# Feed-forward on blocks of 1024 tokens: seven products of halves, and the second product with the weights stationary

## The chip, the cores and the metric

The kernel runs on one core of a Trainium2 chip. The core has a matmul engine (PE, with its weight loads shown as PEld), a vector engine (DVE), a scalar engine (ACT), a general engine (POOL), an engine that issues most of the DMA transfers (SP), and 16 DMA engines. The metric is device time in microseconds (us).

## The reference

Three layers follow each other: an attention with squared ReLU, a mixture of eight experts of which each token takes one, and a feed-forward. Only the last is changed:

```python
def _moe2_ref(x, w_in, w_out):            # x: 24576 x 256, w_in: 256 x 2048, w_out: 2048 x 256
    h = x @ w_in
    g = h * (1.0 / (1.0 + np.exp(-h)))
    return (g @ w_out).astype(np.float32)
```

## The kernel before

The work runs in three stages: attention, experts, feed-forward. Within a stage the order of the instructions is written by hand, as a loop over iterations g in which each engine's instructions are recorded in the order in which they are to run. An engine takes its instructions in that order. Waits between engines are put in by the tile layer, which tracks who read and wrote a tile.

A number is kept as the sum of a high part, rounded to the matmul's format (fp32r), and a low part, the rest. A product of two such numbers is taken as three products: high x high, high x low, low x high. `split` (line 147) makes the two parts: ACT copies, DVE subtracts.

The feed-forward takes blocks of 512 tokens (CB) and, in each iteration, 256 of the 2048 columns of the first product; a block has 8 iterations, the stage 48 x 8 = 384. `emit_H` (line 903) multiplies: for each of two groups of 128 columns and each of two halves of the inner dimension of 256, three matmuls of 512 columns (lines 911 to 913), with a weight as the stationary operand. The result stands in PSUM, tile `hps`. `elem_c` (line 1122) computes the sigmoid on ACT, the product with it on DVE, the high part on ACT and the low part on DVE, each over 1024 columns at once. `emit_AV_c` (line 1132) multiplies by the second weight: here the activations are the stationary operand, and high and low weight lie side by side, so a matmul of 512 columns (lines 236, 239) gives the products with both; the low activations take matmuls of 256 columns (237, 238). The first product runs two iterations ahead of the second (`pipeline_c`, line 1092), and eight PSUM banks hold two `hps` tiles of two banks and four accumulators.

`load_c` (line 1112) loads a block of the input by four DMAs on SP's queue in pieces of 256 bytes, `tr_x` (858) transposes it on DVE, `ev_x` (866) splits it, all several iterations ahead. `evac_c` (line 1137) adds the two halves of an accumulator, and SP stores the block by one DMA.

The second weights arrive as 64-bit numbers; `plan_cw` (line 980) converts both weights to high and low parts during the expert stage, one or two instructions in an iteration, into tiles with pads between them (`CPAD`).

Of the kernel before, what the change touches and what calls it, by code (L numbers as in the profile page):

```python
# [20 lines left out]
def relu2_attention__moe_top1__silu_ffn_kernel(  # L21
# [12 lines left out]
):  # L34

# [43 lines left out]
    CB = 512  # L79
    CT = CB // P  # L80
    NCB = N // CB
    GP = DFF // P // 2

# [43 lines left out]
    X2 = nc.dram_tensor("x2_scratch", (N, D), F32, kind="Internal").ap()  # L127
    TS = [nc.dram_tensor(f"ts{i}_scratch", (P, 2 * QN), F32, kind="Internal").ap() for i in range(3)]
# [95 lines left out]
    def at(g, fn):  # L224
        bg.setdefault(g, []).append(fn)
# [740 lines left out]
    CPAD = (0, 64, 224, 192)  # L966

    def start_c():

        only_a.close()  # L970
        pool = cw["pool"] = ctx.enter_context(tc.tile_pool(name="poolC", bufs=1))
        cw["wih"], cw["wil"], cw["wo"] = [], [], []
        for q in range(4):
            if CPAD[q]:
                pool.tile([P, CPAD[q] // 4], F32, name=f"cpad{q}")
            cw["wih"].append(pool.tile([P, KD, DFF // 4], F32R, name=f"wih{q}"))
            cw["wil"].append(pool.tile([P, KD, DFF // 4], F32R, name=f"wil{q}"))
            cw["wo"].append(pool.tile([P, DFF // P // 4, 2, D], F32R, name=f"wo{q}"))

    def plan_cw(g, src, dst):  # L980
# [10 lines left out]
        def hi(d=I32):  # L991
            return h["raw"].bitcast(d)[:, :, :, 1]
# [7 lines left out]
        def field():  # L1000
# [30 lines left out]
    def plan_cws(g):  # L1031
        for i in range(GP):
            q, o = divmod(i, GP // 4)
            fs = slice(o * 2 * P, (o + 1) * 2 * P)
            cs = slice(2 * o, 2 * o + 2)
            plan_cw(g, w_in_v[:, :, i * 2 * P:(i + 1) * 2 * P, :],
                    lambda q=q, fs=fs: (cw["wih"][q][:, :, fs], cw["wil"][q][:, :, fs]))
            plan_cw(g + 6, w_out_v[:, 2 * i:2 * i + 2],
                    lambda q=q, cs=cs: (cw["wo"][q][:, cs, 0, :], cw["wo"][q][:, cs, 1, :]))
            g += 12  # L1040

    NAB = NIT + NIB
    plan_cws(NIT + 24)
# [48 lines left out]
    def pipeline_c(lo, hi):  # L1092
        g = min(bg)
        while g < hi:
            ahead = g + 2 if lo <= g + 2 < hi else None
            if ahead is not None:
                s = emit_S_c(ahead)
            run(bg, g)
            if g >= lo:
                emit_AV_c(g)  # L1100
            if ahead is not None:
                rest = elem_c(ahead, s)
            if g >= lo:
                evac_c(g)
            if ahead is not None:
                rest()
            g += 1


    XC = {}  # L1110

    def load_c(b):
        XC[b] = mt("y", [P, 4 * CT, 64], F32, "xc")
        load_rows(XC[b], CT, X2[b * CB:(b + 1) * CB])

    def emit_S_c(g):
        b, i = divmod(g, GP)
        q, o = divmod(i, GP // 4)
        fs = slice(o * 2 * P, (o + 1) * 2 * P)
        return emit_H(XT[b], cw["wih"][q][:, :, fs], cw["wil"][q][:, :, fs], CB)  # L1120

    def elem_c(g, ps):
        s = mt("r1", [P, 2, CB], F32, "sg")
        a = mt("r2", [P, 2, CB], F32, "ga")
        A.activation(out=s, in_=ps, func=AF.Sigmoid)  # L1125
        V.tensor_tensor(out=a, in0=ps, in1=s, op=ALU.mult)  # L1126
        h = hi_t[g] = mt("h", [P, 2, CB], F32R, "gh")
        l = lo_t[g] = mt("l", [P, 2, CB], F32R, "gl")
        A.activation(out=h, in_=a, func=AF.Copy)  # L1129
        return lambda: V.tensor_tensor(out=l, in0=a, in1=h.bitcast(F32), op=ALU.subtract)  # L1130

    def emit_AV_c(g):
        b, i = divmod(g, GP)
        q, o = divmod(i, GP // 4)
        emit_acc(g, CT, [flat(cw["wo"][q], 2 * o + f) for f in range(2)], i == 0, i == GP - 1)

    def evac_c(g):
        b, i = divmod(g, GP)
        if i < GP - 1:
            return  # L1140
        o = mt("u", [P, CT, D], F32, "oc")
        for j in range(CT):
            acc = acc_t.pop(j)
            t1 = mt("t1", [P, D], F32, "t1")
            A.activation(out=t1, in_=acc[:, D:2 * D], func=AF.Copy)
            V.tensor_tensor(out=o[:, j], in0=acc[:, 0:D], in1=t1, op=ALU.add)
        SP.dma_start(out=out[b * CB:(b + 1) * CB].rearrange("(j p) d -> p j d", p=P), in_=o)

    with tc.manual_schedule():
# [8 lines left out]
        for b in range(NCB):  # L1158
            g = b * GP
            at(g - 10, lambda b=b: load_c(b))  # L1160
            at(g - 6, lambda b=b: tr_x(XC.pop(b), CT, b, by=KD if b else 1))
            at(g - 5, lambda b=b: ev_x(CT, b, KD if b else 1))
        pipeline_c(0, NCB * GP)
# [32 lines left out]
```

## Time and profile before

| | |
|---|---|
| median of three runs | 5356.03 us (5354.76 to 5363.61) |
| the profiled execution | 5354.29 us, span 5352.3 us |
| attention / experts / feed-forward start at about | 0 / 2034 / 3208 us |
| PE busy in the span | 99% |
| DVE, ACT busy in the span | 65%, 57% |
| feed-forward: first matmul, last matmul | 3208.27, 5346.91 us |

Times are from the span's start. A matmul's shown length includes its way through the engine, so matmuls overlap; what one costs PE is the distance from its start to the start of the next. "Idle before" names what ended an engine's wait.

### The profile page before, as it was taken

The page shows a single profiled execution, that of the slowest core. Times are in us where ns is not written, and L with a number is a line of the kernel's source. Part 1 is how long each engine was busy: PE and PEld are TensorE (multiplying, and loading weights), DVE is VectorE, ACT ScalarE, POOL GpSimd, SP SyncE. Part 2 cuts the span into 40 slices and gives each one's busy share as a digit, 9 for nine tenths or more (in the row PEclk, how much of TensorE's full clock was granted, in tenths as well). Part 3 has the DMA queues.
Part 4 walks back from the last instruction along what each step waited for, and adds up shares of the span by engine and source line. Part 5 has one row for each costly group of instructions (what it writes and reads, how often), then busy time and mean ns, then how long its engine had stood idle before and what let it go on. Part 6 is the DMA issues. An engine that isn't in the chain of part 4 may idle for free.

```text
span 5352.3 us, 77144 instructions
## 1 busy us (share of the span) xinstructions
PE 5280.5 (99%) x29600; PEld 4589.1 (86%) x29600; DVE 3496.2 (65%) x4352; ACT 3055.0 (57%) x4010; POOL 752.1 (14%) x977
## 2 busy tenths in 40 slices
PE   8999999999999999999999999999999999999999
PEld 7888889898989897888888888888888888888888
DVE  6777777777786878777766665555555555555554
ACT  7777777777777875555555554444444444444444
POOL 1131322222222313111111120000000000000000
PEclk9999999999999999999999999999999999999999
DMA  5556565556565556655544550000000000000000
GB/s 149 174 171 182 167 186 165 177 169 185 170 177 172 175 176 190 179 160 160 158 141 142 142 150 17 24 24 24 24 24 24 24 24 24 24 24 24 24 24 20
DMA packets 711601, 588.06 MB, mean 110 GB/s; under 512 B 372892, under 2 KB 629951, under 8 KB 711232
## 3 DMA queue, kind: packets, MB, share of 16 engines
q1 hardware_dynamic: 539200, 458.63, 28.8%
q10 hardware_dynamic: 152928, 73.95, 5.5%
q0 software_dynamic: 19104, 50.56, 2.6%
q8 instruction: 231, 3.78, 0.3%
q14 instruction: 138, 1.13, 0.1%
HBM read 364.89 MB, written 207.59 MB: 107 GB/s over the span
## 4 chain that ended last, share of the span: by engine, by line
PE 69%; issue 17%; DMA 7%; ACT 2%; DVE 2%; POOL 2%; SPq 1%; ACTq 0%; POOLq 0%; DVEq 0%
PE acc L236 11%; PE acc L239 11%; PE hps L912 7%; PE hps L911 7%; PE hps L913 7%; PE acc L238 6%; PE acc L237 6%; PE acct L697 4%; PE acct L698 4%; PE acct L699 4%; DMA x_scratch<-y,gi 2%; DMA ts_scratch<-tb 2%; PE s L642 2%; PE s L643 2%; DMA at<-ts_scratch 2%
## 5 line engine op out<-in xcount | busy, mean ns | idle before, releaser
L1126 DVE TENSOR_TENSOR ga<-hps,sg 128x1024 f32<-128x1024 f32 x384 | 470.3, 1225 | 578.0 <-ACT sg L1125 578.0
L1125 ACT ACTIVATE sg<-hps 128x1024 f32<-128x1024 f32 x384 | 394.5, 1027 | 739.8 <-PE hps L913 739.8
L1130 DVE TENSOR_TENSOR gl<-ga,gh 128x1024 fp32r<-128x1024 f32 x384 | 470.1, 1224 | 379.8 <-ACT gh L1129 379.8
L1129 ACT ACTIVATE gh<-ga 128x1024 fp32r<-128x1024 f32 x384 | 407.3, 1061 | 496.2 <-DVE ga L1126 496.2
L911 PE MATMUL hps<-xh,wih 128*128 128x512 f32 x1536 | 605.8, 394 | 10.0 <-ACT xh L148 10.0
L913 PE MATMUL hps<-xh,wil 128*128 128x512 f32 x1536 | 605.9, 394 | 0.0
L912 PE MATMUL hps<-xl,wih 128*128 128x512 f32 x1536 | 605.9, 394 | 0.0
L236 PE MATMUL acc<-wo,gh 128*128 128x512 f32 x1536 | 604.4, 394 | 0.0
L239 PE MATMUL acc<-wo,gh 128*128 128x512 f32 x1536 | 602.8, 392 | 0.0
L697 PE MATMUL acct<-vs,th 128*128 128x256 f32 x1920 | 542.9, 283 | 17.8 <-DVE xg L704 17.0
L698 PE MATMUL acct<-vs,th 128*128 128x256 f32 x1920 | 541.8, 282 | 0.0
L699 PE MATMUL acct<-vs,tl 128*128 128x256 f32 x1920 | 541.4, 282 | 0.0
L239 PE MATMUL acc<-vs,ah 128*128 128x512 f32 x1344 | 532.8, 396 | 0.0
L236 PE MATMUL acc<-vs,ah 128*128 128x512 f32 x1344 | 532.3, 396 | 0.0
L664 DVE TENSOR_TENSOR al<-a,ah 128x1024 fp32r<-128x1024 f32 x336 | 408.9, 1217 | 107.4 <-ACT ah L657 104.4
L651 ACT ACTIVATE a<-s 128x1024 f32<-128x1024 f32 x336 | 342.5, 1019 | 185.0 <-PE s L643 160.8
L238 PE MATMUL acc<-wo,gl 128*128 128x256 f32 x1536 | 429.8, 280 | 0.0
L237 PE MATMUL acc<-wo,gl 128*128 128x256 f32 x1536 | 428.6, 279 | 0.0
L927 ACT ACTIVATE hh<-hps 128x1024 fp32r<-128x1024 f32 (+1 forms) x220 | 213.9, 972 | 343.6 <-PE hps L913 295.9
L928 DVE SCALAR_TENSOR_TENSOR hl<-hps,hh 128x1024 fp32r<-128x1024 f32 (+1 forms) x220 | 254.3, 1156 | 231.1 <-ACT hh L927 229.3
L662 DVE STREAM_TRANSPOSE tb<-a 128x1024 f32<-128x1024 f32 x240 | 297.5, 1240 | 133.1 <-ACT a L653 130.0
L697 PEld LDWEIGHTS acct<-vs,th 128*128 128x128 f32 x1920 | 364.9, 190 | 22.3 <-DVE xg L704 21.1
(224 smaller groups left out, 13053.0 us busy)
## 6 DMA issues: line engine op xcount, KB each, us to landing
ts_scratch<-tb SPq DMA_DIRECT2D x240, 512.0 KB
at<-ts_scratch SPq DMA_DIRECT2D x960, 128.0 KB
r<-in_moe_w_dram SPq DMA_DIRECT2D x220, 512.0 KB
vr<-in_v_dram ACTq DMA_DIRECT2D x48, 512.0 KB
ut<-in_u_dram ACTq DMA_DIRECT2D x48, 512.0 KB
xb<-xs_scratch SPq DMA_DIRECT2D x192, 128.0 KB
xc<-x_scratch SPq DMA_DIRECT2D x192, 128.0 KB
out_dram<-oc SPq DMA_DIRECT2D x48, 512.0 KB
```

Of the source, the lines that this page charges most:

```text
L236: T.matmul(acc, lhsT=hs[0], rhs=ws[0], start=start, stop=False)
L237: T.matmul(acc[:, D:2 * D], lhsT=ls[0], rhs=ws[0][:, 0:D], start=False, stop=False)
L238: T.matmul(acc[:, D:2 * D], lhsT=ls[1], rhs=ws[1][:, 0:D], start=False, stop=False)
L239: T.matmul(acc, lhsT=hs[1], rhs=ws[1], start=False, stop=stop)
L697: T.matmul(acc[:, kk], lhsT=lh, rhs=vq[:, 0], start=(q == 0), stop=False)
L698: T.matmul(acc[:, kk], lhsT=lh, rhs=vq[:, 1], start=False, stop=False)
L699: T.matmul(acc[:, kk], lhsT=ll, rhs=vq[:, 0], start=False, stop=(q == QT - 1))
L911: T.matmul(o, lhsT=a, rhs=xh[:, d], start=(d == 0), stop=False)
L912: T.matmul(o, lhsT=a, rhs=xl[:, d], start=False, stop=False)
L913: T.matmul(o, lhsT=wl[:, d, f * P:(f + 1) * P], rhs=xh[:, d], start=False, stop=(d == KD - 1))
L1126: V.tensor_tensor(out=a, in0=ps, in1=s, op=ALU.mult)
L1130: return lambda: V.tensor_tensor(out=l, in0=a, in1=h.bitcast(F32), op=ALU.subtract)
```

## The change

The feed-forward takes blocks of 1024 tokens as two halves of 512 (index t), the 2048 columns as two halves of 1024, and the inner dimension as two halves of 128. The first product is then a product of 2 x 2 matrices of blocks, and is taken by seven products of sums instead of eight. With A for the weight's quarters and B for the input's:

- S1 = A21 + A22, S2 = S1 - A11, S3 = A11 - A21, S4 = A12 - S2 for the weight; T1 = B12 - B11, T2 = B22 - T1, T3 = B22 - B12, T4 = B21 - T2 for the input;
- M1 = A11 B11, M2 = A12 B21, M6 = S2 T2, M7 = S3 T3, M5 = S1 T1, M3 = S4 B22, M4 = A22 T4, each three matmuls of 512 columns (`emit_M`);
- H11 = M1 + M2; H22 = M1 + M6 + M5 + M7; H12 = M1 + M6 + M5 + M3; H21 = M1 + M6 + M7 + M4. M1, M6, M5 and M3 add up in one PSUM bank, Q; ACT copies what stands there on the way (`copy`, C[0] to C[2]), and DVE adds a copy to the bank R (M2) or Z (M7, then M4).

An iteration, called a step below, does this for 1024 tokens and 128 columns out of each half, and the second products of the step before; there are 24 x 8 = 192 steps. Q is one half of the tile `m0`, the other half in the next step; R and Z are the halves of the tile `m1`. The eight banks are these four and four accumulators. Sigmoid, product, high and low part are now taken of each 512-column quarter (H11, H22, H21, H12) apart.

The second product takes the weight as the stationary operand and the activations as the moving one, so its result is transposed: six matmuls of 512 columns for each quarter, into accumulators of 128 output columns by 512 tokens. `evac_c` transposes them out of PSUM on DVE, and eight DMAs a block store pieces of 256 bytes. The input's sums, transposes and splits for the next block are spread over a block's eight steps (`prep_c`). The weight's sums are computed in the expert stage after the conversions (`plan_sums`); S2, S3 and S4 go through memory into tiles that the expert stage has done with. The pads between the weights are gone.

```diff
-    CB = 512
-    CT = CB // P
+    CB = 1024
+    CH = CB // 2
...
+    def plan_sums(g):
...
+            def add(x, k):
+                o = h[x] = mt("a", [P, FH], F32R, f"s{x}") if k == 1 else h[x]
+                first = quarter(x, terms[0][1]) if k == 1 else o
+                V.tensor_tensor(out=o.bitcast(F32), in0=first.bitcast(F32), in1=quarter(x, terms[k][1]).bitcast(F32),
+                                op=ALU.add if terms[k][0] > 0 else ALU.subtract)
...
+            ops = [lambda x=x, k=k: add(x, k) for k in range(1, len(terms)) for x in range(2)]
+            for op in [*ops, high, rest, low_part, *([store] if to else [])]:
+                at(g, op)
+                g += 1
...
-    def emit_S_c(g):
+    def prep_c(b):
+
+        return [[], [lambda: load_c(b)], [lambda: tr_c(b, 0), lambda: tr_c(b, 1)],
+                [lambda: sum_c(0), lambda: sum_c(1)], [lambda: sum_c(2), lambda: sum_c(3)],
+                [lambda: parts_c(b, 1)], [lambda: parts_c(b, 2)], [lambda: parts_c(b, 0)], [lambda: parts_c(b, 3)]]
...
+    def emit_M(g, name, o, start=True):
...
+        T.matmul(o, lhsT=wh, rhs=xh, start=start, stop=False, skip_group_check=True)
+        T.matmul(o, lhsT=wh, rhs=xl, start=False, stop=False, skip_group_check=True)
+        T.matmul(o, lhsT=wl, rhs=xh, start=False, stop=True, skip_group_check=True)
...
+        for d in range(2):
...
+            o = acc_c[b, d, t]
+            wh, wl = (cw["o"][:, f * GP + i, y, d * P:(d + 1) * P] for y in range(2))
+            T.matmul(o, lhsT=wh, rhs=x[:, 0], start=start, stop=False)
+            T.matmul(o, lhsT=wh, rhs=x[:, 1], start=False, stop=False)
+            T.matmul(o, lhsT=wl, rhs=x[:, 0], start=False, stop=stop)
...
+    def pipeline_c():
+        s0 = psS.tile([P, 2, CH], F32, tag="s0", name="m0", bufs=1)
+        s1 = psS.tile([P, 2, CH], F32, tag="s1", name="m1", bufs=1)
...
+            Q, R, Z = s0[:, g % 2], s1[:, 0], s1[:, 1]
...
+            if now:
+                emit_M(g, "M1", Q)
+            if old:
+                high(g - 1, "H12")
+                low_part(g - 1, "H22")
+            if now:
+                copy(0, Q)
+                emit_M(g, "M2", R)
+            if old:
+                low_part(g - 1, "H12")
+                mul("H21")
+                high(g - 1, "H21")
+            if now:
+                add("H11", 0, R)
+            if old:
+                low_part(g - 1, "H21")
+                emit_AV_c(g - 1, "H11")
+            if now:
+                sig("H11")
+                mul("H11")
+                emit_M(g, "M6", Q, False)
+                copy(1, Q)
+                high(g, "H11")
+                emit_M(g, "M7", Z)
+            for fn in todo:
+                fn()
+            if now:
+                low_part(g, "H11")
+            if old:
+                emit_AV_c(g - 1, "H22")
+            if now:
+                emit_M(g, "M5", Q, False)
+                copy(2, Q)
+            if old:
+                emit_AV_c(g - 1, "H21")
+            if now:
+                add("H22", 2, Z)
+                sig("H22")
+                emit_M(g, "M3", Q, False)
+                emit_M(g, "M4", Z, False)
+            if end:
+                evac_c(b - 1, 0, 0)
+            if now:
+                sig("H12", Q)
+                mul("H22")
+                high(g, "H22")
+            if end:
+                evac_c(b - 1, 0, 1)
+            if now:
+                add("H21", 1, Z)
+                mul("H12", Q)
+                sig("H21")
+            if old:
+                emit_AV_c(g - 1, "H12")
```

PE's instructions before, in the middle of the feed-forward, at the end of a second product and the start of a first one; names with numbers are single tiles, and the bracket names the engine whose semaphore the instruction waits for:

```order
L237 MATMUL acc_48704<-wo2_24244,gl_48802 128x256
L238 MATMUL acc_48704<-wo2_24244,gl_48802 128x256
L239 MATMUL acc_48704<-wo2_24244,gh_48801 128x512
L911 MATMUL hps_48883<-xh_48493,wih3_24246 128x512 [waits DVE_49]
L912 MATMUL hps_48883<-xl_48494,wih3_24246 128x512
L913 MATMUL hps_48883<-xh_48493,wil3_24247 128x512
```

The first product's tile had been read by DVE an iteration earlier. Now PE's instructions at the end of a step in the middle of the feed-forward: M4, the second products of H12 of the step before, and M1 of the next step.

```order
L1207 MATMUL m1_35699<-xp_41915,wih_24234 128x512 [waits DVE_49]
L1208 MATMUL m1_35699<-xp_41916,wih_24234 128x512
L1209 MATMUL m1_35699<-xp_41915,wil_24235 128x512
L1233 MATMUL acc_42017<-g_42208,wo_24236 128x512
L1234 MATMUL acc_42017<-g_42208,wo_24236 128x512
L1235 MATMUL acc_42017<-g_42208,wo_24236 128x512
L1233 MATMUL acc_42021<-g_42208,wo_24236 128x512
L1234 MATMUL acc_42021<-g_42208,wo_24236 128x512
L1235 MATMUL acc_42021<-g_42208,wo_24236 128x512
L1207 MATMUL m0_35698<-xp_41840,wih_24234 128x512 [waits DVE_49]
L1208 MATMUL m0_35698<-xp_41841,wih_24234 128x512
L1209 MATMUL m0_35698<-xp_41840,wil_24235 128x512
```

M1 in the tenth row waits for DVE; the value of the semaphore that it waits for is reached by DVE's product for H12 (line 1273, out of `m0`), the fourth row of the next piece. DVE's instructions before, in the middle of the feed-forward:

```order
L1126 TENSOR_TENSOR ga_47747<-hps_47713,sg_47746 128x1024 [waits Activation_49]
L1130 TENSOR_TENSOR gl_47751<-ga_47747,gh_47750 128x1024 [waits Activation_49]
L1126 TENSOR_TENSOR ga_47784<-hps_47754,sg_47783 128x1024 [waits Activation_49]
L1130 TENSOR_TENSOR gl_47788<-ga_47784,gh_47787 128x1024 [waits Activation_49]
L862 STREAM_TRANSPOSE xt_47804<-xc_47633 128x16x2x32 [waits DMAHW6_49,DMAHW5_49,DMAHW7_49,DMAHW1_49,DMAHW0_49]
```

And now, from M5 of the same step to the sum for H11 of the next: the sum for H22, its product with the sigmoid, the sum for H21, the product for H12, two low parts, the product for H21, the sum for H11.

```order
L1267 TENSOR_TENSOR hs_35701<-m1_35699,hs_35700 128x512 [waits Activation_49]
L1273 TENSOR_TENSOR sg_35705<-hs_35701,sg_35705 128x512 [waits Activation_49]
L1267 TENSOR_TENSOR hs_35700<-m1_35699,c_35703 128x512 [waits PE_49]
L1273 TENSOR_TENSOR sg_35707<-m0_35698,sg_35707 128x512 [waits Activation_49]
L1283 TENSOR_TENSOR g_42268<-sg_35705,g_42268 128x512 [waits Activation_49]
L1283 TENSOR_TENSOR g_42282<-sg_35707,g_42282 128x512 [waits Activation_49]
L1273 TENSOR_TENSOR sg_35706<-hs_35700,sg_35706 128x512
L1267 TENSOR_TENSOR hs_35701<-m1_35699,c_35702 128x512 [waits PE_49,Activation_49]
```

Two instructions of 1024 columns in an iteration have become eleven of 512 in a step, and the sum for H21 (third row) waits for M4.

## Rows read from the trace of the kernel before

**Rows 1.** The page: busy time of the engines, and shares of the chain:
```profile
PE 5280.5 (99%) x29600; PEld 4589.1 (86%) x29600; DVE 3496.2 (65%) x4352; ACT 3055.0 (57%) x4010; POOL 752.1 (14%) x977
...
PE 69%; issue 17%; DMA 7%; ACT 2%; DVE 2%; POOL 2%; SPq 1%; ACTq 0%; POOLq 0%; DVEq 0%
```

**Rows 2.** Windows: feed-forward, experts, experts later; us, busy us by engine:
```profile
core 0: us, PE busy (x) PEld busy (x) DVE busy (x) ACT busy (x) POOL busy (x), PEclk, DMA share, GB/s
4000.00:5000.00 1000.00, 1000.00 (x5033) 843.37 (x5033) 520.98 (x496) 421.26 (x474) 0.00 (x0) 1.00 0.09 24
2560.00:2920.00 360.00, 360.00 (x1834) 306.24 (x1833) 253.28 (x349) 190.19 (x287) 66.23 (x64) 1.00 0.52 149
2740.00:2900.00 160.00, 160.00 (x815) 136.09 (x814) 99.39 (x130) 81.55 (x122) 28.43 (x28) 1.00 0.49 139
```

**Rows 3.** Timeline of PE in the feed-forward: start us, us, what:
```profile
4000.75 0.39 PE L911 MATMUL hps<-xh,wih 128*128 128x512 f32 x1
...
4003.32 0.39 PE L913 MATMUL hps<-xh,wil 128*128 128x512 f32 x1
4003.55 0.40 PE L236 MATMUL acc<-wo,gh 128*128 128x512 f32 x1
...
4006.33 0.39 PE L911 MATMUL hps<-xh,wih 128*128 128x512 f32 x1
```

**Rows 4.** Timeline of ACT and DVE in the same stretch:
```profile
4003.81 1.03 ACT L1125 ACTIVATE sg<-hps 128x1024 f32<-128x1024 f32 x1 [2.20 <-PE hps L913]
4004.87 1.23 DVE L1126 TENSOR_TENSOR ga<-hps,sg 128x1024 f32<-128x1024 f32 x1 [2.00 <-ACT sg L1125]
4006.12 1.06 ACT L1129 ACTIVATE gh<-ga 128x1024 fp32r<-128x1024 f32 x1 [1.29 <-DVE ga L1126]
4007.22 1.23 DVE L1130 TENSOR_TENSOR gl<-ga,gh 128x1024 fp32r<-128x1024 f32 x1 [1.13 <-ACT gh L1129]
```

**Rows 5.** Groups by form on DVE: count | busy us, mean ns | idle before:
```profile
L704 DVE TENSOR_TENSOR xg<-xg,acct 128x512 f32<-128x512 f32 x240 | 164.0, 684 | 110.7 <-PE acct L699 94.0 <-PE acct L499 11.3 <-PE acct L583 4.0
L149 DVE TENSOR_TENSOR w1l<-r,w1h 128x512 fp32r<-128x512 f32 x220 | 150.7, 685 | 1.2 <-ACT w1h L148 0.9
L862 DVE STREAM_TRANSPOSE xt<-xc 128x1024 f32<-128x1024 f32 x47 | 58.1, 1237 | 0.0
```

**Rows 6.** Groups by form on ACT:
```profile
L148 ACT ACTIVATE w1h<-r 128x512 fp32r<-128x512 f32 x220 | 137.1, 623 | 1.9 <-DMA r<-in_moe_w_dram 1.9
```

**Rows 7.** Timeline of DVE in the expert stage, back to back:
```profile
3170.50 0.69 DVE L149 TENSOR_TENSOR w1l<-r,w1h 128x512 fp32r<-128x512 f32 x1
3171.10 0.69 DVE L149 TENSOR_TENSOR w<-r,w 128x512 fp32r<-128x512 f32 x1
```

**Rows 8.** Timeline of ACT in the expert stage, back to back:
```profile
3169.51 0.62 ACT L148 ACTIVATE w1h<-r 128x512 fp32r<-128x512 f32 x1
3170.03 0.62 ACT L148 ACTIVATE w<-r 128x512 fp32r<-128x512 f32 x1
```

**Rows 9.** Timeline at the end of the feed-forward, PE and ACT:
```profile
5345.51 0.39 PE L239 MATMUL acc<-wo,gh 128*128 128x512 f32 x1
5345.94 0.38 ACT L1145 ACTIVATE t<-acc 128x256 f32<-128x256 f32 x1 [0.32 <-PE acc L239]
```

**Rows 10.** Timeline of the attention, DVE and PE, where PE waits:
```profile
510.65 0.68 DVE L704 TENSOR_TENSOR xg<-xg,acct 128x512 f32<-128x512 f32 x1
...
511.38 0.39 PE L697 MATMUL acct<-vs,th 128*128 128x256 f32 x1 [1.58 <-DVE xg L704]
511.60 0.28 PE L698 MATMUL acct<-vs,th 128*128 128x256 f32 x1
511.72 0.27 PE L699 MATMUL acct<-vs,tl 128*128 128x256 f32 x1
...
794.75 0.50 PE L642 MATMUL s<-st 128*128 128x512 f32 x1 [1.82 <-ACT a L651]
795.08 0.40 PE L643 MATMUL s<-sw,st 128*128 128x512 f32 x1
```

**Rows 11.** Windows: first load of the feed-forward, a store and a load:
```profile
3203.00:3212.00 9.00, 3.73 (x8) 2.71 (x9) 2.60 (x4) 1.22 (x2) 0.00 (x0) 0.50 0.77 175
3308.00:3314.00 6.00, 6.00 (x32) 5.03 (x31) 3.43 (x3) 2.16 (x3) 0.00 (x0) 1.00 0.67 178
```

**Rows 12.** Timeline at the start of the feed-forward:
```profile
3206.84 1.30 DVE L862 STREAM_TRANSPOSE xt<-xc 128x512 f32<-128x512 f32 x2 [7.55 <-DMA xc<-x_scratch]
...
3208.27 0.79 PE L911 MATMUL hps<-xh,wih 128*128 128x512 f32 x1 [10.00 <-ACT xh L148]
...
3211.30 0.63 PE L911 MATMUL hps<-xh,wih 128*128 128x512 f32 x1
3211.72 0.63 PE L912 MATMUL hps<-xl,wih 128*128 128x512 f32 x1
```

**Rows 13.** Timeline at the end, PE and SP:
```profile
5346.91 0.39 PE L239 MATMUL acc<-wo,gh 128*128 128x512 f32 x1
5348.21 0.37 SPq L1147 DMA_DIRECT2D out_dram<-oc  x1
```

More of the change, by code (lines that the diff above doesn't have):

```diff
@@ L964, in relu2_attention__moe_top1__silu_ffn_kernel @@
     cw = {}
-    CPAD = (0, 64, 224, 192)
     def start_c():
@@ L1090, in pipeline_ab @@
             g += 1
[L1092 to L1107, printed above, removed]
@@ L1132, in emit_AV_c @@
-    def emit_AV_c(g):
-        b, i = divmod(g, GP)
[L1134 to L1147, printed above, removed]
+    XC, XF, TC = {}, {}, {}
@@ new lines, in parts_c @@
+    def parts_c(b, n):
+        if n == 3:
+            h, l = (mt("st", [P, CH], F32R, "xp", x) for x in range(2))
+        elif n == 1:
+            h, l = (mt("a" if b % 2 == 0 else "xh", [P, KD, CH], F32R, "xp") for x in range(2))
+        else:
+            h, l = (mt("w2" if n else "xl", [P, KD, CH], F32R, "xp", 2 * (n and b % 2) + x) for x in range(2))
+        split(h, l, TC[n])
+        if n == 3:
+            XF["T4"] = h, l
+        else:
+            for k, name in enumerate((("B11", "B21"), ("T3", "B22"), ("T1", "T2"))[n]):
+                XF[b % 2 if n else 0, name] = h[:, k], l[:, k]
@@ new lines, in relu2_attention__moe_top1__silu_ffn_kernel, with rooms_c, emit_AV_c @@
+    QUADS = dict(H11=(0, 0), H22=(1, 1), H21=(1, 0), H12=(0, 1))
+    quads, acc_c, out_c, room = {}, {}, {}, {}
+    def rooms_c():
+        x, y = mt("w2", [P, 2, CH], F32, "hs", 4), mt("u", [P, 2, CH], F32, "hs", 2)
+        room["H"] = dict(H11=y[:, 0], H22=y[:, 1], H21=x[:, 1])
+        room["c"] = [*(mt("st", [P, CH], F32, "c", 6 + i) for i in range(2)), x[:, 0]]
+        room["a"] = {q: mt("st", [P, CH], F32, "sg", 2 + i) for i, q in enumerate(QUADS)}
+    def emit_AV_c(g, q):
+        b, i = divmod(g, GP)
+        f, t = QUADS[q]
+        x = quads.pop((g, q))
+        start = i == 0 and q in ("H11", "H22")
+        stop = i == GP - 1 and q in ("H21", "H12")
+        for d in range(2):
+            if start:
+                acc_c[b, d, t] = psA.tile([P, CH], F32, tag="acc", name="acc")
+            o = acc_c[b, d, t]
[3 more added lines that the diff above has]
+            T.matmul(o, lhsT=wl, rhs=x[:, 0], start=False, stop=stop)
@@ new lines, in evac_c @@
+    def evac_c(b, t, d):
+        if d == 0:
+            out_c[t] = mt("u", [P, CH // 32, 64], F32, "oc", t)
+        o = out_c[t]
+        V.transpose(out=o.rearrange("p j (r k) -> p j k r", k=2)[:, :, d],
+                    in_=acc_c.pop((b, d, t)).rearrange("p (j c) -> p j c", c=32))
+        if d == 1:
+            rows = out[b * CB + t * CH:b * CB + (t + 1) * CH]
+            for i in range(4):
+                SP.dma_start(out=rows[:, 64 * i:64 * i + 64].rearrange("(j c) m -> c j m", c=32),
+                             in_=o[32 * i:32 * i + 32])
@@ L1157, in relu2_attention__moe_top1__silu_ffn_kernel @@
         A.activation(out=ess, in_=ess, func=AF.Sigmoid)
[L1158 to L1163, printed above, removed]
+        load_c(0)
+        tr_c(0, 0)
+        parts_c(0, 0)
+        tr_c(0, 1)
+        for n, p in ((0, None), (2, 2), (1, 1), (3, None)):
+            sum_c(n)
+            if p:
+                parts_c(0, p)
+        pipeline_c()
 _INS = ['u', 'v', 'z', 'moe_expert_emb', 'moe_tau', 'moe_w1', 'moe_w2', 'moe2_w_in', 'moe2_w_out']
```

131 lines of the change are left out of this document (99 added, 32 removed).

## Prediction

> **What bounds the kernel now.** I read the page first: PE is busy in 99% of the span, DVE in 65%, ACT in 57%, and the chain that ended last is mostly PE [rows 1]. Then the windows, because an average over three stages says little about the one that is changed. The change lies in the last stage, the feed-forward. In 1000 us of it PE is busy all the time at full clock, DVE 521 us, ACT 421 us, and 5033 matmuls run [rows 2]. An iteration (512 tokens, 256 columns of the first product) has 28 matmuls, 20 of 512 columns and 8 of 256, so it takes 1000 x 28/5033 = 5.563 us. That is 24 units of 512 columns, so a unit is 5.563/24 = 0.2318 us; call it a. The timeline shows the same: the first product starts at 4000.75, the second at 4003.55, the next iteration at 4006.33 [rows 3]. ACT and DVE work in that time on four instructions of 1024 columns with idle time between them [rows 4]. So the stage costs 384 x 5.563 = 2136 us, all of it PE's columns; nothing else is late there.
>
> **What the change removes.** For 1024 tokens and 256 columns of the first product (one step; before two iterations) PE had 2 x 24 = 48 units, 11.13 us. Now it has seven products of three units and four second products of six units: 21 + 24 = 45 units, 45 x 0.2318 = 10.43 us. Over 192 steps columns alone would save 192 x 0.70 = 134 us. The unit may move, since all operands lie elsewhere in memory now: the middle stage, with the same 28 matmuls in an iteration, shows 360 x 28/1834/24 = 0.2290 [rows 2]. I keep 0.2318 and take 0.2290 to 0.2345 (as far above as below) for the range.
>
> **What it adds on ACT and DVE.** A 512-column instruction takes 0.69 us on DVE (684 and 685 ns) and 0.62 on ACT [rows 5, 6]; back to back they start every 0.60 and 0.52 [rows 7, 8]. A step has eleven of each: on DVE 11 x 0.60 = 6.6 us, where two iterations had four of 1.22. Each block of eight steps adds on DVE two transposes (1.24 each), four differences, three splits of 1024 and one of 512 columns, and four transposes out of PSUM (not shown before; I take 0.69, like other 512-column work): about 12 us, 1.5 a step. DVE is then some 8.1 of 10.4 us busy, ACT less. Neither is the bound by its sum. So the order decides.
>
> **Where the order bites.** The PE rows of the new order show the first matmul of each step, M1, waiting for DVE. It writes one half of m0, while the last DVE instruction on m0 of the step before, the product for H12, reads the other half: the wait goes by the tile. Behind M1 everything on PE is queued. The path from one M1 to the next: PE runs M1 to M4 with three second products between, 39 units = 9.04 us. DVE may start on M4's result 0.43 us after the start of its last matmul (ACT did so at the end of the last stage: 5345.51 to 5345.94 [rows 9]), 0.20 after its unit. The sum for H21 runs, and 0.60 later the product for H12 starts, 0.69 us long. PE then starts 0.05 us after DVE's end (510.65 + 0.68 = 511.33, PE at 511.38), and a matmul that has waited holds the next one up: 0.22 instead of 0.12 behind it at 511.38, 0.33 instead of 0.23 at 794.75 [rows 10], so 0.11 more. Sum: 9.04 + 0.20 + 0.60 + 0.69 + 0.05 + 0.11 = 10.69 us, against 10.43 of columns. That wait is what is late next, 0.26 a step. Bounds: 10.43 if something on the path is shorter, and each handover 0.06 more if a second semaphore stands ahead (0.49 from 4003.32 to 4003.81 [rows 3, 4]).
>
> The 0.60 is weighed once. DVE's rows start 0.60 apart though each lasts 0.69 [rows 7]. The Trainium skill (VectorE: DVE Perf Modes, "The DRAIN you can't avoid") says that the next instruction does not start until the pipe is empty; by that the term would be 0.69, the step 10.78, and the forecast 5331. The trace disagrees by 0.09, and I go by the trace.
>
> The rest of the step, worked forward from M1 at 0 with the same durations and 0.03 us between DVE and ACT: DVE does low parts and the product for H21 until 1.8 us, the sum for H11 until 2.5, ACT its sigmoid until 3.2, DVE the product until 3.9; ACT copies M6's result (there at 3.7) until 4.3 and rounds H11 until 4.8, DVE's low part ends at 5.5. M5's result is there at 6.45: ACT's copy ends at 7.1, DVE's sum for H22 at 7.85, the sigmoid at 8.5, the product at 9.2, just as M4's result comes (9.24). M4 itself waits for the sum for H22, 7.85 + 0.05, and PE reaches it at 8.3: 0.4 us of slack.
>
> Three steps of a block split 1024 columns ahead of the low part of H11: ACT's copy ends at 5.8, DVE's subtraction at 7.0, the low part at 7.6, and what follows the sum for H22 is 0.27 later at H21: 10.96. In a block's first step a transpose out of PSUM stands ahead of the sum for H21, 0.50 more: 11.19. The step that transposes the input has 2.3 us more on DVE; from 3.8 to 7.16 us DVE had only one low part to do (0.60), so 2.7 us are free: nothing. A block: 4 x 10.69 + 3 x 10.96 + 11.19 = 86.8 us, before 16 x 5.563 = 89.0. Gain 2.2 us a block, 24 blocks: 52.6 us.
>
> **Ends.** The first product waited for the load until 3206.84, then DVE and ACT on half tiles, until 3208.27; PE's clock had fallen to its 1.2 GHz level in the wait, and matmuls came every 0.43 [rows 11, 12]. Now transposition and copy take 1024 columns: 1 us later. The first step has no second products, and PE waits for transposes, differences and splits (about 11 us to the seventh product, 17 in all): 6 us more than a normal step. At the end a step with second products alone, 24 units and small waits: 5.8 us. The last block prepares nothing: -0.8. The tail of stores is 5.2 us from the last matmul's unit to the end [rows 13] and about the same now. Together +12.
>
> **Before the last stage.** The sums of the weights are 18 DVE and 4 ACT instructions of 1024 columns, one in an iteration of 5.5 us. Between 2740 and 2900 us DVE is busy 99 of 160 us and PE all of it [rows 2], and up to 2740, with one or two more conversions in each iteration, PE was just as full; I cost it at nothing. Without that cover it would be 18 x 1.22 = 22 us.
>
> **DMA.** Stores go out in pieces of 256 B instead of 1 KB, and in a block's first step 1 MB of them stands on SP's queue ahead of 1 MB of loads for the next block. Loads of such pieces ran at 175 GB/s [rows 11]. At that rate all 2 MB have landed 11 to 12 us after the first step; DVE needs the first half of the loads at 14.6 (10.7 of the second step and 3.9 of the third) and the rest at 15.7. I take nothing. No row shows a store in small pieces; rival 3 prices that.
>
> **Sum.** 5354.3 of the profiled execution (its span is 5352.3) - 52.6 + 12 = 5314 us. The median of the runs is 5356, 0.03% above, so 5314 stands. A difference under 0.2% (11 us) I call none.
>
> **Rivals.** (1) M1 is not late: then 10.43 a step, about 5232; partly, anywhere up to 5290. For it: the path exceeds the columns by only 0.26 us, made of six small terms. Against it: each is a row. (2) Handovers cost more than the rows show, since nearly every instruction of a step waits for another engine: 0.2 us more a step takes back 38 us, 5352, no change; slower from 0.28 on. For it: before, ACT and DVE ran four instructions in 5.5 us [rows 4], now 22 in 10.7, nearly each behind the other engine. (3) Slower: small stores. In the third step of each block the two transposes stand on DVE ahead of the low part of H11 and the sum for H22, for which M4 waits. The second transpose may start 5.75 us into that step before M4 is late, so stores may take 11.4 us ahead of 6 us of loads. At half of the loads' rate (88 GB/s) they take 12, 0.65 us late, 23 times 15 us: 5329. At a third 18, 6.5 us late, 150 us: 5464. Below about 80 GB/s it decides for slower. Against it: stores of 1 KB and loads together ran at 178 GB/s over 6 us [rows 11], and loads need not wait for the last store. The Trainium skill (DMA: Bandwidth & Descriptors, "Specifications") asks for 512 B or more for line rate and speaks of read-modify-write below. Taken as twice the bytes, an estimate from that page, it would be the 5329; no run here shows it yet. (4) It doesn't give the columns back: pads between the weights are gone, and if a rises above 0.237 the 39 units take all of the gain, 5354 or more. Rows show 0.2290 and 0.2318, so this is far.
>
> **Chances.** Forecast 0.60 with its own range 5288 to 5340 (a from 0.2290 to 0.2345 is -21 to +20, the 0.11 lost or kept -21); rival 1 0.11; rival 2 0.14; rival 3 0.09; rival 4 0.06. The range reaches into rivals 1 and 2: 5258 to 5368. Faster: 0.60 + 0.11 + 0.04 of rivals 2 and 4 = 0.75; same 0.09; slower 0.16.
>
> **What would show it.** Steps of 10.7 us with PE idle some 0.15 us before M1, put down to DVE's product for H12; 10.96 in three steps of eight; 512-column matmuls every 0.23. PE busy throughout and 10.4 a step would prove rival 1; PE idle at M4 in the third step with DVE waiting for a load, rival 3; idle time at M7, M5 or M3 as well, rival 2. An idle PE before 3200 us would prove the sums of the weights wrong.

## The result: 5298.6 us, 1.1% less than before

The changed kernel took 5298.62 us (median of 4 runs, 5294.56 to 5301.98) against 5357.15 for the kernel before (4 runs): a ratio of 0.9889 (95% interval 0.9871 to 0.9906). Forecast was 5314, faster; the time is 15 us below it and inside the likeliest case's own range. The profiled execution took 5294.56, its span is 5292.8, against 5354.29 and 5352.3.

In the profile after, the page's busy times and chain (to be read beside [rows 1]) show PE at 98% instead of 99%, DVE and ACT busier, and more of both on the chain (15% instead of 4%):

```profile
PE 5180.2 (98%) x27488; PEld 4389.7 (83%) x27488; DVE 4019.0 (76%) x5760; ACT 3501.1 (66%) x5213; POOL 750.0 (14%) x977
...
PE 65%; issue 11%; DVE 9%; ACT 6%; DMA 6%; POOL 1%; SPq 1%; ACTq 0%; POOLq 0%; DVEq 0%
```

The windows of [rows 2], of after (the same stretches of the feed-forward and of the experts), and PE's waits in the first of them (who waited <- for whom: us in all, times, longest):

```profile
core 0: us, PE busy (x) PEld busy (x) DVE busy (x) ACT busy (x) POOL busy (x), PEclk, DMA share, GB/s
4000.00:5000.00 1000.00, 983.67 (x4185) 774.53 (x4184) 782.13 (x1187) 646.18 (x1068) 0.00 (x0) 1.00 0.11 26
2560.00:2920.00 360.00, 360.00 (x1831) 306.14 (x1830) 272.77 (x366) 194.76 (x290) 67.63 (x64) 1.00 0.53 153
2740.00:2900.00 160.00, 160.00 (x816) 136.14 (x815) 115.90 (x144) 84.64 (x127) 29.25 (x28) 1.00 0.52 152
```

```profile
PE m L1207 <- DVE sg L1273: 15.3, 45, 0.6
```

In the feed-forward the view lists one wait of PE: its first matmul of a product (L1207) for the product with the sigmoid on DVE (L1273), 45 times in the 93 steps of this window. In the other steps the matmul before M1 still shows as busy when M1 starts late, and the same holds for short waits at M4 and M7: the view does not count them, the timeline shows them. In the expert stage PE stays full, though DVE does 19.5 us more of work in 360 (253.28 before, 272.77 now): the sums of the weights cost nothing. The last expert matmul starts at 3195.80, 2.1 us earlier than before (3197.87).

PE's timeline over a plain step (M1 at 4032.85 to the next at 4043.37) and a split step, one of the three in a block that split 1024 columns of the next block's input (to 4054.27); start, length, what, and in brackets idle time before:

```profile
4032.85 0.50 PE L1207 MATMUL m<-xp,wih 128*128 128x512 f32 x1
4033.19 0.39 PE L1208 MATMUL m<-xp,wih 128*128 128x512 f32 x1
...
4041.61 0.39 PE L1209 MATMUL m<-xp,wil 128*128 128x512 f32 x1
...
4042.97 0.39 PE L1235 MATMUL acc<-g,wo 128*128 128x512 f32 x1
4043.37 0.50 PE L1207 MATMUL m<-xp,wih 128*128 128x512 f32 x1
4043.71 0.40 PE L1208 MATMUL m<-xp,wih 128*128 128x512 f32 x1
...
4051.44 0.39 PE L1209 MATMUL m<-xp,s 128*128 128x512 f32 x1
4051.69 0.50 PE L1207 MATMUL m<-xp,wih 128*128 128x512 f32 x1
4052.03 0.40 PE L1208 MATMUL m<-xp,wih 128*128 128x512 f32 x1
...
4054.27 0.50 PE L1207 MATMUL m<-xp,wih 128*128 128x512 f32 x1 [0.25 <-DVE sg L1273]
```

DVE's, at the plain step's end (sum for H21, product for H12) and in the split step (subtraction of the split, low part of H11, sum for H22):

```profile
4042.03 0.69 DVE L1267 TENSOR_TENSOR hs<-m,c 128x512 f32<-128x512 f32 x1
4042.64 0.68 DVE L1273 TENSOR_TENSOR sg<-m,sg 128x512 f32<-128x512 f32 x1
...
4049.20 1.23 DVE L152 TENSOR_TENSOR xp<-xs,xp 128x1024 fp32r<-128x1024 f32 x1 [1.90 <-ACT xp L151]
4050.35 0.68 DVE L1283 TENSOR_TENSOR g<-sg,g 128x512 fp32r<-128x512 f32 x1
4050.95 0.68 DVE L1267 TENSOR_TENSOR hs<-m,hs 128x512 f32<-128x512 f32 x1
```

The path of the prediction stands here link by link. M4's last matmul starts at 4041.61. The sum starts 0.42 later, the product 0.61 after the sum though the sum lasts 0.69, it ends at 4043.32, M1 starts 0.05 later at 4043.37, 0.40 behind the matmul before it instead of 0.23, and the next one follows after 0.34. A plain step is 10.52 us (forecast 10.69), a split step 10.90 (10.96), a block's first 11.08 (11.19; means of 22 blocks). In the split step M4 (4051.69) also waits, for the sum for H22, which ends at 4051.63.

What differs from the forecast is the spacing. From 4033.19 to 4041.61 are 37 matmuls in 8.42 us: 0.2276. Averaged over the stage, without the gaps, it is 0.2278; the forecast had 0.2318 from [rows 2]. With 0.2278, 39 units are 8.88, and the forecast's own sum gives 8.88 + 0.20 + 0.60 + 0.69 + 0.05 + 0.11 = 10.53, measured 10.52. So the question for the experiments is twofold: where the closer matmuls come from, and whether the wait at M1 is the false one (another half of the same tile) that the prediction took it for.

### The profile page after: what moved, and what is told of

It is laid out like the page before. It is cut to its first block, busy times and chain, and to the rows that moved or that the text cites. A ratio compares the mean times of both kernels' runs of the same rounds, so it can differ in the third digit from the quotient of the medians.

```text
span 5292.8 us, 76091 instructions
## 1 busy us (share of the span) xinstructions
PE 5180.2 (98%) x27488; PEld 4389.7 (83%) x27488; DVE 4019.0 (76%) x5760; ACT 3501.1 (66%) x5213; POOL 750.0 (14%) x977
## 4 chain that ended last, share of the span: by engine, by line
PE 65%; issue 11%; DVE 9%; ACT 6%; DMA 6%; POOL 1%; SPq 1%; ACTq 0%; POOLq 0%; DVEq 0%
PE acc L242 6%; PE acc L239 6%; PE m L1207 5%; PE m L1209 4%; PE m L1208 4%; PE acc L1234 4%; PE acc L1233 4%; PE acc L1235 4%; PE acct L700 4%; PE acct L701 4%; PE acct L702 4%; PE acc L241 3%; PE acc L240 3%; PE s L645 2%; PE s L646 2%
## 5 line engine op out<-in xcount | busy, mean ns | idle before, releaser
L1233 PE MATMUL acc<-g,wo 128*128 128x512 f32 x1536 | 598.9, 390 | 0.0
L1234 PE MATMUL acc<-g,wo 128*128 128x512 f32 x1536 | 598.2, 389 | 0.2 <-DVE g L1283 0.2
L1235 PE MATMUL acc<-g,wo 128*128 128x512 f32 x1536 | 597.7, 389 | 0.0
L1279 ACT ACTIVATE g<-sg 128x512 fp32r<-128x512 f32 x768 | 484.1, 630 | 133.2 <-DVE sg L1273 120.2
L1283 DVE TENSOR_TENSOR g<-sg,g 128x512 fp32r<-128x512 f32 x768 | 524.4, 685 | 59.1 <-ACT g L1279 23.9
L1270 ACT ACTIVATE sg<-hs 128x512 f32<-128x512 f32 x576 | 364.2, 632 | 202.6 <-DVE hs L1267 194.0
L1273 DVE TENSOR_TENSOR sg<-hs,sg 128x512 f32<-128x512 f32 x576 | 395.9, 687 | 120.9 <-ACT sg L1270 118.7
L679 ACT ACTIVATE th<-at 128x1024 fp32r<-128x1024 f32 x240 | 253.4, 1056 | 230.7 <-PE acct L701 130.2
L700 PEld LDWEIGHTS acct<-vs,th 128*128 128x128 f32 x1920 | 364.9, 190 | 18.8 <-DVE xg L707 17.6
L241 PE MATMUL acc<-vs,al 128*128 128x256 f32 x1344 | 375.4, 279 | 0.0
L701 PEld LDWEIGHTS acct<-vs,th 128*128 128x128 f32 x1920 | 365.6, 190 | 10.2
L240 PE MATMUL acc<-vs,al 128*128 128x256 f32 x1344 | 374.1, 278 | 0.0
```

Of the source, the lines that this page charges most:

```text
L240: T.matmul(acc[:, D:2 * D], lhsT=ls[0], rhs=ws[0][:, 0:D], start=False, stop=False)
L241: T.matmul(acc[:, D:2 * D], lhsT=ls[1], rhs=ws[1][:, 0:D], start=False, stop=False)
L700: T.matmul(acc[:, kk], lhsT=lh, rhs=vq[:, 0], start=(q == 0), stop=False)
L701: T.matmul(acc[:, kk], lhsT=lh, rhs=vq[:, 1], start=False, stop=False)
L1233: T.matmul(o, lhsT=wh, rhs=x[:, 0], start=start, stop=False)
L1234: T.matmul(o, lhsT=wh, rhs=x[:, 1], start=False, stop=False)
```

## Experiments: what each part is worth

Times are compared with the kernel before, run on the same chip (5350.7 us, 5345.11 to 5356.90, for the four first kernels timed, 5353.0 for the later ones).

**The kernel before without the pads.** In before's trace the first product's spacing depends on the quarter of the weights: 0.2275 in the first, 0.2330 to 0.2334 in the three others (means over the iterations; [rows 3] show one of these three: 4000.75 to 4003.55 are 12 matmuls of 0.2333). The change took the pads away.

```diff
-    CPAD = (0, 64, 224, 192)
+    CPAD = (0, 0, 0, 0)
```

> The kernel before with its weights' tiles of the feed-forward one behind another, without the 64, 224 and 192 bytes between the four quarters. In it the first product's matmuls started 0.2271 to 0.2281 us apart for the first quarter of the weights and 0.2325 to 0.2334 for the other three; in the changed kernel 0.2278 throughout. Theory A (the address of the weights sets the spacing): the spacing in quarters two to four changes by several ns, to 0.227 if the first quarter's offset is the good one: 288 iterations x 12 units x 0.0055 = 19 us less, 5337; more if the old ones were the good ones. Theory B (the matmuls of 256 columns in the second product set the rate of what follows): nothing moves, 5351 to 5361.

Measured: 5328.35 us, ratio 0.9958 (0.9944 to 0.9971). One iteration's first product, from its first matmul to the first of the second product:

```profile
4005.35 0.39 PE L911 MATMUL hps<-xh,wih 128*128 128x512 f32 x1
...
4008.08 0.39 PE L236 MATMUL acc<-wo,gh 128*128 128x512 f32 x1
```

These are 12 matmuls in 2.73; the mean is 0.2270 in every quarter. The second product kept its 0.2319. Theory A holds: taking the pads away is worth 22 us here.

**The kernel before with stationary weights in the second product.**

```diff
+            for f in range(2):
+                wh, wl = (cw["wo"][q][:, 2 * o + f, y, d * P:(d + 1) * P] for y in range(2))
+                T.matmul(acc_c[d], lhsT=wh, rhs=h[:, f], start=i == 0 and f == 0, stop=False)
+                T.matmul(acc_c[d], lhsT=wh, rhs=l[:, f], start=False, stop=False)
+                T.matmul(acc_c[d], lhsT=wl, rhs=h[:, f], start=False, stop=i == GP - 1 and f == 1)
```

> The kernel before with the second half of the change alone: second product with the weights stationary, 12 matmuls of 512 columns instead of 8 of 512 and 8 of 256, results transposed by DVE out of PSUM and stored in pieces of 256 bytes; the first product stays at eight products of halves (12 matmuls of 512 columns in an iteration). The columns stay the same, 24 units in an iteration. Theory B (the 256-column matmuls make the unit long): the unit falls from 0.2318 to 0.2270 to 0.2280 us throughout: 384 x 24 x 0.0038 to 0.0048 = 35 to 44 us less, 5312 to 5321. Theory A (where the weights lie makes it long): only the second product changes, by up to 0.003 x 12 units x 384 = 14 us, 5342 to 5356, and quarters two to four of the first product keep 0.233. Small stores (rival 3 of the prediction): if pieces of 256 bytes are slow, DVE waits for loads and PE with it, 15 us or more on top.

Measured: 5355.46 us, ratio 1.0008 (0.9999 to 1.0017), no change. The first product keeps its spacing (0.2275 in the first quarter, 0.2329 to 0.2334 in the others), and the second, now with the weights as the stationary operand, follows the same pattern: 0.2294 in the first quarter, 0.2328 to 0.2335 in the others. Theory B falls.

**Both: no pads, and stationary weights.** All of the change but the seven products and the longer blocks that they need.

> The kernel before without the pads and with the second product's weights stationary, that is all of the change but the seven products in place of eight. Without the pads alone the time was 5328, with stationary weights alone 5355. Theory (the place of the weights sets the spacing, in the second product too once they are the stationary side): all 24 units of an iteration at 0.2270, 384 x 12 x 0.005 = 23 us less than 5328, 5305. That would be as fast as the whole change, whose three units less a step would then have gone into the waits. Rival (the two parts don't add up, the second product stays at 0.232): 5328 to 5332.

Measured: 5304.91 us, ratio 0.9909 (0.9894 to 0.9925). Timeline: first product from 4000.51, second from 4003.23, next iteration at 4005.95, 12 matmuls in 2.72 each, 0.2267 throughout:

```profile
4000.51 0.39 PE L911 MATMUL hps<-xh,wih 128*128 128x512 f32 x1
...
4003.23 0.39 PE L1144 MATMUL acc<-gh,wo 128*128 128x512 f32 x1
...
4005.95 0.39 PE L911 MATMUL hps<-xh,wih 128*128 128x512 f32 x1
```

As the theory expected. Its interval overlaps that of the whole change (0.9871 to 0.9906): against a kernel with weights as well placed, seven products instead of eight have gained nothing that these runs can tell. The traces say why. Two iterations here take 2 x 5.44 = 10.88 us and have no wait; a step of the changed kernel takes 86.07/8 = 10.76 on average. Three units less are 0.68, of which the waits take back 0.56; 192 x 0.12 is 23 us, less the 13 of the ends (below).

**The changed kernel with 64 bytes ahead of its weights.**

```diff
+        pool.tile([P, 16], F32, name="cpad")
         cw["i"] = [pool.tile([P, 2, KD, FH], F32R, name=f"wi{x}") for x in "hl"]
```

> The changed kernel with 64 bytes put ahead of its weights, so that they lie where the second quarter of the kernel before lay; all else as it is. Theory (the forecast's unit of 0.2318 was too long because the change also took the pads away): 36 of the 45 units of a step read these weights (the sums of halves lie elsewhere), 192 x 36 x 0.0055 = 38 us more than 5299, 5337; matmuls after the wait settle at 0.232 to 0.233. Rival (the changed kernel's matmuls are closer for another reason, such as the order of the products): 0.2266 to 0.228 as before, 5299.

Measured: 5325.31 us, ratio 0.9945 (0.9932 to 0.9959). M1 in two plain steps following each other:

```profile
4122.69 0.50 PE L1208 MATMUL m<-xp,wih 128*128 128x512 f32 x1
...
4133.40 0.50 PE L1208 MATMUL m<-xp,wih 128*128 128x512 f32 x1
```

10.71 us apart. The mean spacing is 0.2328, the steps 10.72 plain, 10.96 split, 11.21 first, the block 87.1: with the pad the forecast of 10.69, 10.96, 11.19 and 86.8 is met. The time rose by some 30 us (5.6 thousandths of the ratio) and not by 38, because in a split step DVE's path to M4 sets the pace and longer units only fill PE's wait: those steps grew by 0.06 instead of 0.20.

**Which offsets do harm.** The kernel before with other pads, one run of each; what is read from it is the spacing within the run.

```diff
-    CPAD = (0, 64, 224, 192)
+    CPAD = (0, 32, 96, 128)
```

> The kernel before with pads of 0, 32, 96 and 128 bytes ahead of the four quarters of the feed-forward's weights: the quarters lie 0, 32, 128 and 256 bytes further than without pads. Offsets of 64, 288 and 480 bytes took 0.2333 us a matmul of the first product, offset 0 took 0.2270. The theory (the place of the weights sets the spacing) expects some quarters at 0.2270 and others at 0.233 in one kernel, and the run tells which offsets do no harm: if a multiple of 128 bytes is good, quarters three and four are at 0.2270 and quarter two at 0.233; if only 256 is, quarter four alone; if neither, all three are at 0.233. Rival (any pad in the pool does it, wherever the weights then lie): quarters two to four are at 0.233.

Measured: 5347.83 us (before 5350.45). The first product in an iteration of the second, third, fourth and first quarter:

```profile
4013.84 0.40 PE L911 MATMUL hps<-xh,wih 128*128 128x512 f32 x1
4016.64 0.39 PE L236 MATMUL acc<-wo,gh 128*128 128x512 f32 x1
...
4025.01 0.40 PE L911 MATMUL hps<-xh,wih 128*128 128x512 f32 x1
4027.81 0.40 PE L236 MATMUL acc<-wo,gh 128*128 128x512 f32 x1
...
4036.17 0.39 PE L911 MATMUL hps<-xh,wih 128*128 128x512 f32 x1
4038.90 0.40 PE L236 MATMUL acc<-wo,gh 128*128 128x512 f32 x1
...
4047.24 0.39 PE L911 MATMUL hps<-xh,wih 128*128 128x512 f32 x1
4049.97 0.39 PE L236 MATMUL acc<-wo,gh 128*128 128x512 f32 x1
```

2.80, 2.80, 2.73 and 2.73 us. Offsets of 32 and 128 bytes widen the spacing, 256 is as good as 0: with either the matmuls settle at 0.2267 from the fifth of an iteration on, while with 32 and 128 they go up and down around 0.233 to its end. It is the place, not the pad: the quarter 256 bytes on has three pads ahead of it. The 64, 288 and 480 of the kernel before widen the spacing too, so of the offsets tried only 0 and 256 did no harm. 512 has no number: a version with offsets of 0, 128, 256 and 512 needs more memory than is left. Why the place matters, no run shows.

## Experiments: the wait at M1

**The order on DVE swapped.**

```diff
-                add("H21", 1, Z)
                 mul("H12", Q)
+                add("H21", 1, Z)
                 sig("H21")
```

> Theory (M1 waits for the product for H12 because it writes the other half of the same tile m0): with the product for H12 put ahead of the sum for H21 on DVE, it no longer has 0.60 us of another sum between M4's result and itself, ends before PE reaches M1, and M1 starts in the normal spacing of 0.23 us. But the sum for H21 and what hangs on it come 0.60 later, DVE reaches the sum for H11 of the next step later by as much, and M7, which writes the other half of the tile m1 that this sum reads, is late in M1's place: by 0.3 to 0.4 us, a step of 10.45 to 10.6, 5290 to 5305 us, no change against 5299. Rival (the excess of 0.3 us a step belongs to the wait for the product itself, and M7 has slack): the wait at M1 goes and none takes its place, a step of 10.25 us, 5299 - 180 x 0.3 = 5245.

Measured: 5300.77 us, ratio 0.9907 (0.9892 to 0.9922), no change. M1 follows in the normal 0.23 in seven steps of eight. In the step behind a block's end M7 waits, for a sum on DVE (the idle time is in brackets):

```profile
4004.39 0.39 PE L1209 MATMUL m<-xp,s 128*128 128x512 f32 x1
4005.24 0.50 PE L1207 MATMUL m<-xp,s 128*128 128x512 f32 x1 [0.46 <-DVE hs L1267]
4005.58 0.40 PE L1208 MATMUL m<-xp,s 128*128 128x512 f32 x1
```

In plain steps M7 costs less than expected, 0.08 to 0.28 us with the hold of the matmul behind it, and they take 10.30 to 10.54. But the split steps rose to 11.02 to 11.23, with M4 0.79 instead of 0.25 behind its predecessor, and the block is 86.5 against 86.1 (means of 22 blocks). The theory had the new place of the wait right and missed M4. The rival (5245) is out: 0.60 us later on DVE makes the next matmuls late.

**Four tiles of one bank each.** The same instructions in the same order; only the tracking changes.

```diff
-        s0 = psS.tile([P, 2, CH], F32, tag="s0", name="m0", bufs=1)
-        s1 = psS.tile([P, 2, CH], F32, tag="s1", name="m1", bufs=1)
+        only_ab.close()
+        psC = ctx.enter_context(tc.tile_pool(name="psC", bufs=1, space=PSUM))
+        q0, q1, rr, zz = (psC.tile([P, CH], F32, tag=t, name=t, bufs=1) for t in ("q0", "q1", "rr", "zz"))
...
-            Q, R, Z = s0[:, g % 2], s1[:, 0], s1[:, 1]
+            Q, R, Z = (q0, q1)[g % 2][:, :], rr[:, :], zz[:, :]
```

> Four tiles of one PSUM bank each instead of two tiles of two halves; the same instructions in the same order. Theory (both waits go by the tile, and nothing but the two shared tiles holds PE up in a plain step): M1's wait for the product for H12 and M7's for the sum for H11 vanish, a plain step is 45 units of 0.2268 to 0.2278, 10.2 to 10.25 us, with no wait of PE; split steps keep M4's wait for the sum for H22 in part, 10.2 to 10.6. Together about 75 us less than 5299: 5215 to 5235. Rival (the wait at M1 is one for the handovers DVE to PE in general: the true needs of M3 to M4, or of the second products, are as late): M1's wait goes and another takes its place at M4, at a second product or at M5, a step of 10.4 to 10.5, 5280 to 5300.

Measured: 5218.97 us, ratio 0.9753 (0.9740 to 0.9766), 1.4% below the changed kernel's ratio. The window of before, and PE's only wait in it:

```profile
4000.00:5000.00 1000.00, 996.38 (x4343) 811.13 (x4342) 811.83 (x1231) 673.36 (x1111) 0.00 (x0) 1.00 0.11 26
```

```profile
PE zz L1208 <- DVE hs L1269: 2.4, 15, 0.2
```

M1 with its neighbours in a plain step and its next, and M4 in a split step:

```profile
4031.29 0.50 PE L1208 MATMUL zz<-xp,wih 128*128 128x512 f32 x1 [0.16 <-DVE hs L1269]
...
4074.70 0.39 PE L1236 MATMUL acc<-g,wo 128*128 128x512 f32 x1
4074.92 0.39 PE L1208 MATMUL q<-xp,wih 128*128 128x512 f32 x1
4075.15 0.39 PE L1209 MATMUL q<-xp,wih 128*128 128x512 f32 x1
...
4085.12 0.39 PE L1208 MATMUL q<-xp,wih 128*128 128x512 f32 x1
```

A plain step is 10.20 us, 45 x 0.2267, with no wait at all; split steps are 10.42 to 10.65. So the wait at M1 and that at M7 were for data that PE did not need. The Trainium skill (PSUM — Partial Sum Buffer, "PSUM bank collisions raise a hardware error") says to guard PSUM by bank and quadrant; the tracking by a tile of two banks guards more than that, and this run shows what the surplus cost: 0.0136 of the ratio, some 73 us.

**The split behind the low part.** On top of the four tiles, in the three split steps of a block:

```diff
+            if now and i > 4:
+                low_part(g, "H11")
             for fn in todo:
                 fn()
-            if now:
+            if now and i <= 4:
                 low_part(g, "H11")
```

> The version with four tiles of one bank, and in the three split steps of a block the low part of H11 ahead of the splitting of the next block's input on DVE. Theory (M4 is late in these steps because the sum for H22 stands on DVE behind a subtraction that waits for ACT's copy): M4's wait goes, steps 5 to 7 take 10.20 instead of 10.43, 10.65 and 10.65, 23 x 1.12 = 26 us less than 5219, 5193. Rival (ACT's 1024-column copy is what makes the sum late): M4 stays late and the time stays within 5 us of 5219.

Measured: 5190.51 us, ratio 0.9699 (0.9686 to 0.9713), the best version. In the window PE is busy throughout, and M1 comes every 10.20 us in a split step too:

```profile
4000.00:5000.00 1000.00, 1000.00 (x4403) 825.12 (x4402) 830.34 (x1246) 689.97 (x1126) 0.00 (x0) 1.00 0.11 26
```

```profile
4081.76 0.39 PE L1208 MATMUL q<-xp,wih 128*128 128x512 f32 x1
...
4091.96 0.39 PE L1208 MATMUL q<-xp,wih 128*128 128x512 f32 x1
```

Steps 5 to 7 are 10.20 as the theory expected; only the step behind a block's end keeps 0.2 (M5, 0.28 and 0.34 in place of 0.23). The subtraction no longer stands ahead of the low part, and the sum for H22 comes in time.

## Why the prediction was right, point by point

- **What bounds it, and what is late next: right.** PE's columns before; after, the false wait at M1 behind sum and product on DVE. Each of the terms behind the 39 units has its row in the profile after (0.42 from the start of M4's last matmul, which is its unit and 0.19, then 0.61, 0.68, 0.05, 0.11), and the four tiles show that nothing but the shared tiles stood behind it in a plain step.
- **The unit, 0.2318: the term that was mis-sized.** It measured 0.2278 (0.2267 some ten matmuls behind a wait). The forecast averaged over the feed-forward of before. It said that the unit may move, "since all operands lie elsewhere in memory now", and kept the average; it did not look at the quarters apart, where the means (0.2275, and 0.2330 to 0.2334) would have shown it. Effect by the steps: (10.69 - 10.52) x 3 + (10.96 - 10.90) x 3 + 0.11 less 0.03 for the second step is 0.77 a block, 18 us in 24 blocks; the profiled execution came out 19 below the sum. Padded back, the block took 87.1, forecast 86.8. The measured unit also lies outside the bounds that the forecast gave it (0.2290 to 0.2345). By the forecast's own sum it would have taken off 39 x 0.0040 x 192 = 30 us, to 5284, below the range of 5288 to 5340. That the time fell inside is in part luck: M4 in the split steps and M7 behind a block's end came late, which the forecast did not have, and so the steps gave only 18 of these 30.
- **The 0.60 against the pipe's emptying: right.** Sum and product start 0.61 apart (4042.03, 4042.64) with a length of 0.69. The Trainium skill (VectorE: DVE Perf Modes, "The DRAIN you can't avoid") says that the next instruction does not start until the pipe is empty. The same paragraph adds that an instruction that is not held starts earlier, which the prediction left out. By the first sentence alone the step would have been 0.08 longer; no step shows that.
- **Split steps and a block's first step: right within 0.11.** M4 has its 0.4 us of slack in a plain step (the sum for H22 ends at 4040.69, M4 starts at 4041.15). In the split steps the forecast's own 0.27 left 0.17 of it, and the shorter units used that up: PE reaches M4 sooner, waits 0.02 and holds the next by 0.11. With the 64 bytes, where the units are long, M4 is not late. The step behind a block's end, 10.72, has M7 late by 0.05 and 0.11, which the forecast did not have.
- **Ends, +12: right.** The first matmul came 11.13 us behind the expert stage's last (10.40 before), the first step took 18.29 (17 forecast; the granted clock is 0.50 between 3207 and 3227, the 1.2 GHz level), and the stage is 2078.9 us from first to last matmul, 13 above 24 x 86.07. From the last matmul's start (5285.85) to the end are 6.95 us, 1.6 more than before.
- **DMA: nothing, right; rival 3 is out.** Windows behind a block's end, when stores in pieces of 256 B and then loads stand on SP's queue, and the transposes that need the loads:

```profile
4000.00:4005.00 5.00, 4.42 (x19) 3.11 (x18) 4.90 (x9) 2.71 (x5) 0.00 (x0) 1.00 0.72 184
4005.00:4010.00 5.00, 5.00 (x23) 4.13 (x22) 2.58 (x5) 2.81 (x6) 0.00 (x0) 1.00 0.98 226
4010.00:4016.00 6.00, 5.98 (x26) 4.61 (x25) 5.80 (x10) 4.53 (x8) 0.00 (x0) 1.00 0.06 12
```

```profile
4015.65 2.37 DVE L1154 STREAM_TRANSPOSE xs<-xc 128x1024 f32<-128x1024 f32 x2
```

All 2 MB are through shortly after 4010, 5 us before DVE asks for them, at up to 226 GB/s: more than the 175 of [rows 11], not half of it. (That 175 is an average over 9 us in which the DMA engines were busy 0.77 of the time.) The stores are slower than before all the same. The windows within a store of the kernel before, in pieces of 1 KB (one DMA of 512 KB), and of this one, in pieces of 256 B (eight DMAs of 128 KB):

```profile
3309.00:3310.00 1.00, 1.00 (x8) 0.89 (x7) 0.59 (x1) 0.38 (x1) 0.00 (x0) 1.00 1.01 353
4001.00:4004.00 3.00, 2.92 (x13) 2.40 (x14) 3.00 (x7) 1.30 (x3) 0.00 (x0) 1.00 0.84 215
```

The Trainium skill (DMA: Bandwidth & Descriptors, "Specifications") asks for 512 B or more for line rate. The traces agree in the direction: 353 GB/s with the DMA engines busy throughout, 215 at a share of 0.84, which would be 256 at full share (an estimate from that row). How much of the rest comes from the pieces and how much from eight DMAs in place of one, no run tells apart. Within the stage the slower stores cost no time, since nothing waited for them.

- **Rivals 1, 2 and 4.** M1 was late (1 is out). No handover cost more than its row (2 is out; two semaphores ahead did not show on this path). The unit fell instead of rising (4 has the right cause, the place, and the wrong sign).

By the ratios, the 59 us of gain divide into 22 for the pads, 26 for stationary weights at a good place in the second product, and 11, no more than the intervals' width, for the seven products. Another 102 lay in the tracking of the tiles (73) and in the order of the split steps (29). The division hangs on the order in which the parts are taken: with the weights 64 bytes on, the change still gained 28 us, and stationary weights beside the pads gained nothing, so at that spacing the seven products are worth some 28 us and not 11. What they save in columns comes out only when the waits are gone: the best version (0.9699) is 112 us shorter than the one with eight products, no pads and stationary weights (0.9909), of the 192 x 3 x 0.2267 = 131 us that three units a step are worth.

## What to carry to other kernels

Before a unit is averaged over a stage, read it apart by operand: a matmul's spacing differed by 3% with the place of its weights, which was worth most of the change's effect (up to 48 of 59 us). Where an engine waits for an instruction that reads another half of a tile, give the halves tiles of their own before reordering anything: swapping two instructions only moved the wait to the next shared tile. A change that takes work off the bound by a few per cent has to be read together with the longest path through the other engines, which is late next.

## What the runs showed of the hardware that was not expected

- The matmuls' spacing depends on where the stationary weights lie: 0.2267 to 0.2270 us with all of them at the unpadded places; beside quarters at offsets of 32, 64, 128, 288 or 480 bytes, which took 0.2323 to 0.2337, those at 0 or 256 took 0.2270 to 0.2281.
- After a wait the spacing begins at 0.232 to 0.235 and falls to 0.2267 within some ten matmuls; the matmul right behind the one that waited comes 0.11 later than that (0.34).
- Without pads the second product of the kernel before (activations stationary, weights moving) kept 0.2319 a unit; with the weights stationary it took 0.2267. What makes the former longer is open.
- Stores in pieces of 256 B, as eight DMAs of 128 KB, ran at 215 GB/s, in pieces of 1 KB, as one DMA of 512 KB, at 353. Which of the two differences counts for more is open.
